# Scores of four heads in one TensorE block, a hidden layer in two PSUM banks, and V of two heads split at once

## The chip, the cores and the metric

One NeuronCore of a Trainium2 chip runs one program. The metric is the time of one execution on the device in microseconds (us). The engines that matter are TensorE (PE, with its weight loads as PEld), VectorE (DVE), ScalarE (ACT) and the sync engine (SP), which issues nearly all the DMAs. A matmul's result lands in PSUM, which has eight banks of 512 fp32 columns on each of 128 partitions.

## The reference

```
scores = q @ k.T / 8 + bias(head, distance)     # batch 4, 8 heads, 768 positions, head size 64
scores = where(first n_global keys or the last n_local, scores, -1e9)
x = softmax(scores) @ v                         # (4, 8, 768, 64) -> 3072 tokens x 512
h = x @ w_in                                    # 512 -> 2048
g = max(h, 0) + alpha * min(h, 0)
out = g @ w_out                                 # 2048 -> 512, fp32
```

## The kernel before, in words

**Tiles.** The 3072 tokens are worked off in 12 units `u` of 256 tokens, three to a batch. A unit has attention for 8 heads (`attend`) and the two layers. Keys outside a local window and 32 global columns are never computed: a query block of 128 has 256 key columns, or 128 where it is a batch's first; so a head's scores are two windows of 256 columns, or, in units 0, 3, 6 and 9, one of 128 and one of 256. Each head's scores take one PSUM bank.

**Precision.** Values are split into two fp16 parts (ScalarE or VectorE makes the high part, VectorE the rest), and each product is three fp16 matmuls. From unit 4 on (`QU`) this holds for scores too: one block is 12 matmuls of 64 contraction rows (line 627), two heads at once, one in rows 0 to 63 of the array and one in rows 64 to 127. All other matmuls use all 128 rows.

**Attention of a head.** Scores; bias, mask and row minimum in one VectorE instruction per window (line 650); exp on ScalarE (655); probabilities split (`ps`, lines 347/348 and 367); a DMA transposes them into `vp`, the buffer that holds the head's split V as well (697, 699); two heads' values are multiplied in one TensorE block (711) into the bank `av`, four heads to a bank; VectorE scales the four heads into `xn` (722).

**First layer.** From unit 3 on `ff_in4` makes four feature blocks by a Strassen-like scheme: seven products of 12 matmuls (829) into three partial sums X, Y and Z. The order is X (B11), Z (B21), Y (T1), X (T2), Y (B22), X (T3), X (T4). X and Y come from the two `h` banks in turn, Z from the bank `ax`. ScalarE takes copies of X and Y on the way (`take`, 837), VectorE joins Z and Y with copies (`join`, 840), applies alpha (865), and the result is split into `ghl` (872, 366). `ff_out` multiplies it by the second layer's weights (927). Unit 2 uses `ff_in2` instead, which puts two feature blocks in the two halves of one bank (896) and reads each half on its own.

**PSUM.** `sp` 2 banks (scores), `av` 1, `ax` 1, `h` 2, `o` 2: all eight.

**Order.** The program is a static order per engine. Every operation is given to `Plan` with a key (a place in time, counted in slots of which a unit has 16), its reads and writes, and a guessed cost. `Plan.order` simulates the engines: each takes the ready operation with the lowest key whose buffers are free. Operations are emitted in the order of their planned starts, and semaphores are set by the tile framework from that order. Keys that matter: scores of head h at `begin(u) + 2h`, its values at 5.5 after its pair's second head; `ff_in4` at the unit's slot, `ff_out` of block f `GLAG` slots behind. `FLEX` says when an engine takes over another's copy, `OWN` how long the plan lets a result age before the same engine uses it. The plan tracks the parts of a buffer that an operation names as separate.

Of the kernel before, what the change touches and what calls it, by code (L numbers as in the profile page):

```python
# [15 lines left out]
F16 = mybir.dt.float16  # L16
# [7 lines left out]
P = 128  # L24
# [7 lines left out]
UT = 256  # L32
# [7 lines left out]
XS, WI, WO, KG = 2.0**8, 2.0**8, 2.0**8, 2.0**-11  # L40
OSC = 1.0 / (XS * WI * WO * KG)
QS = 2.0**6
# [244 lines left out]
def c_dma(nbytes):  # L287
    return nbytes / 360.0
# [7 lines left out]
WIDE = 1  # L296
KP = 2
DP = 3.5
FLEX = {'ACT': 2, 'DVE': 1.5, 'POOL': 1}
GROUP = (2, 4, 4, 4)  # L300
PT4 = 0
DL = 3
# [6 lines left out]
WARM = 9  # L309
US = 3  # L310
QU = 4
LOADS = 1500
LANDS = 2500
OWN = {'PE': 0, 'DVE': 125}
SIGN = 6
QLEAD = 2
EV = 2
SLEAD = 36
SL = 3
GLAG = 6.5  # L320
SPARE = 600
CHECK = 140
RW = "abcd"
# [4 lines left out]
def fast(tc, cn, a):  # L328
    nc = tc.nc
    ctx = ExitStack()  # L330
    with ctx:
# [7 lines left out]
        def op(eng, key, cost, fn, r=(), w=(), spare=0):  # L339
            plan.op(key, r, w, (eng, cost, fn), spare=spare)  # L340

        def mul(key, out, src, by, r, w, first="ACT", n=None, psum=False):

            tile_ = hasattr(by, "t")
            ways = dict(
                ACT=("ACT", c_act(n, psum, tile_),
                     lambda: nc.scalar.mul(out=out(), in_=src(), mul=by.t if tile_ else by)),  # L347
                DVE=("DVE", c_dve(n, not psum, tile_), lambda: v.tensor_scalar(
                    out=out(), in0=src(), scalar1=by.t if tile_ else by, scalar2=None, op0=ALU.mult)),
            )  # L350
            plan.op(key, r, w, *[ways.pop(e) for e in (first, *[x for x in ways if x != first])])
# [8 lines left out]
        def rest(key, out, src, by, hi, r, w, n, first="DVE"):  # L360

            val = lambda: by.t if hasattr(by, "t") else by

            def on(e):
                if by is None:
                    return e.tensor_tensor(out=out(), in0=src(), in1=hi(), op=ALU.subtract)  # L366
                return e.scalar_tensor_tensor(out=out(), in0=src(), scalar=val(), in1=hi(), op0=ALU.mult,  # L367
                                              op1=ALU.subtract)

            ways = [("DVE", c_dve(n, False, hasattr(by, "t")), lambda: on(v))]  # L370
            if by is None and first == "POOL":
                ways.insert(0, ("POOL", c_pool(n), lambda: on(nc.gpsimd)))
            plan.op(key, r, w, *ways)


        def buf(tag, name, shape, dtype=F32):
            return Buf(plan, pools[tag], tag, shape, dtype, name)
# [159 lines left out]
        first, firstv = {}, {}  # L537
# [25 lines left out]
        def windows(u):  # L563

            if u % 3:
                return ((0, 0, 256, 0, 0), (1, 160, 256, 0, 256))
            return ((0, 0, 128, 256, 0), (1, 32, 256, 0, 128))

        xn, xt_, xt, group, pair, halves = {}, {}, {}, {}, {}, {}

        def scale_bias(h, key):
            op("ACT", key, c_act(384), lambda: nc.scalar.mul(out=Dh[h].t, in_=Dh[h].t, mul=QS**2), r=[], w=[Dh[h]])
# [1 line left out]
        def idle(u, h, tag, *others):  # L574

            return ((tag,) + others)[h % (1 + len(others))] if u == 0 else tag

        def attend(u, h, key):

            b, c = divmod(u, 3)  # L580
            nk = 416 if c else 288
            nb = 4 if c else 3
            nv, npr = 64 * nb, 128 * nb
            plain = u < 2
            late = not plain
            uh = f"{u}_{h}"

            kp = key - KP - (3 if late else 0)
            if u > 1 and h % 2 == 0:

                x = buf("qk", "qk" + uh, [P, 672])
                op("SP", kp - 4, c_dma(P * 4 * (256 + nk)), lambda: nc.sync.dma_start(
                    out=x.t[:, : 256 + nk], in_=a["qk"][u - 2, h // 2, :, : 256 + nk]), w=[x], spare=LOADS)
                y = buf("v", "v" + uh, [P, 512])
                op("SP", kp - 4 + (1 if late else 0), c_dma(P * 8 * nv), lambda: nc.sync.dma_start(
                    out=y.t[:, : 2 * nv], in_=a["vw"][u - 2, :, h * nv : (h + 2) * nv]), w=[y], spare=LOADS)
                for i in range(2):
                    first[u, h + i] = x, (lambda i=i: x.t[64 * i : 64 * i + 64, : 256 + nk])
                    firstv[u, h + i] = y, (lambda i=i: y.t[:, nv * i : nv * i + nv])
            rq, qk_ = first[u, h]  # L600
            rv, vrt = firstv[u, h]
            if u >= QU and h % 2 == 0:
                z = halves[u] = buf("qs", "qs" + uh, [P, 2, 672], F16)
                nq = 256 + nk
                mul(kp + QLEAD, lambda: z.t[:, 0, :nq], lambda: rq.t[:, :nq], QS, [rq], [(z, 0)], "ACT", nq)
                rest(kp + QLEAD, lambda: z.t[:, 1, :nq], lambda: rq.t[:, :nq], QS, lambda: z.t[:, 0, :nq], [rq, (z, 0)],
                     [(z, 1)], nq)
            if late:

                vp = buf("rd", "vp" + uh, [P, 2048], F16)  # L610
                rvh, rvl, rpt = (vp, 0), (vp, 1), (vp, 2)
                vhi, vlo, pflat = (lambda: vp.t[:, :256]), (lambda: vp.t[:, 256:512]), (lambda: vp.t[:, 512:1536])
                vv = lambda: vrt()[:, :nv]
                mul(kp + 3, lambda: vhi()[:, :nv], vv, XS, [rv], [rvh], "ACT", nv)
                rest(kp + 3, lambda: vlo()[:, :nv], vv, XS, lambda: vhi()[:, :nv], [rv, rvh], [rvl], nv)

            n2 = 1 if u == 2 or u == 3 and h < 4 else 2
            if h % n2 == 0:
                pair[u] = two = [buf(idle(u, h + i, "sp", "h"), f"sp{u}_{h + i}", [P, 512]) for i in range(n2)]

                def products(zz=halves.get(u)):
                    z = zz.t
                    for qb, off, n, _, pc in windows(u):
                        for m, (qi, ki) in enumerate(((0, 0), (0, 1), (1, 0))):
                            for i, sp in enumerate(two):
                                rows = slice(64 * i, 64 * i + 64)
                                nc.tensor.matmul(sp.t[:, pc : pc + n], lhsT=z[rows, qi, 128 * qb : 128 * qb + 128],  # L627
                                                 rhs=z[rows, ki, 256 + off : 256 + off + n], start=m == 0, stop=m == 2)

                def scores():  # L630
                    for i, sp in enumerate(two):
                        qk_ = first[u, h + i][1]
                        for qb, off, n, _, pc in windows(u):
                            nc.tensor.matmul(sp.t[:, pc : pc + n], lhsT=qk_()[:, 128 * qb : 128 * qb + 128],  # L634
                                             rhs=qk_()[:, 256 + off : 256 + off + n], start=True, stop=True)

                if u >= QU:
                    op("PE", key, 1.25 * npr + 200, products, r=[halves[u]], w=two)
                else:
                    op("PE", key, 1.67 * npr + 200, scores, r=[rq], w=two)  # L640
            sp = pair[u][h % n2]
# [5 lines left out]
            sm, av, works = group[u]  # L647

            for qb, _, n, dc, pc in windows(u):
# [3 lines left out]
                    r=[sp, Dh[h]], w=[(pr, qb), (sm, (n_, qb))])  # L653
            for qb, _, n, dc, pc in windows(u):
# [4 lines left out]
                    r=[(sm, (n_, qb))], w=[(pr, qb), (sm, (n_, 2 + qb))])  # L659
# [135 lines left out]
                         T2=(pick(a_, 10, 4), (a_, 1)), T3=(pick(b_, 0, 4), b_), T4=(pick(b_, 2, 4), b_),  # L795
                         B22=(pick(c_, 0, 2), c_))

        mo, acc = {}, {}

        def ff_in4(u, f4, key):  # L800

            x = xt[u]
            X, Y, Z = (buf(t, f"h{n}{u}_{f4}", [P, UT]) for t, n in (("h", "x"), ("h", "y"), ("ax", "z")))
            hs = buf("ra", f"hs{u}_{f4}", [P, 4, UT])
            ghl = buf("ra", f"ghl{u}_{f4}", [P, 2, 4 * UT], F16)
            kept = [buf("g", f"g{u}_{f4}_{i}", [P, 2 * UT]) for i in range(2)]
            snap = {n: (kept[i // 2], i % 2) for i, n in enumerate(("m1", "u2", "m5", "u3"))}
            two = lambda t: (t[0].t[:, UT * t[1] : UT * t[1] + UT] if isinstance(t, tuple) else t.t).rearrange(
                "p (q t) -> p q t", q=2)
            into = lambda i, t: hs.t[:, i::2, 128 * t : 128 * t + 128]  # L810

            def plain_w(i, half):
# [4 lines left out]
                return (lambda q, wi, c: sums[2 * f4 + q].t[:, wi, 256 * i + 128 * c : 256 * i + 128 * c + 128],  # L817
                        [(sums[2 * f4 + q], z) for q in range(2) for z in (i // 2, 2 + i // 2)])

            def product(k, bank, weights, name, begin, end):  # L820
                wt, rw = weights
                xp, rx = x[name]

                def go():
                    for q in range(2):
                        n = 0
                        for c in range(2):
                            for wi, xi in ((0, 0), (0, 1), (1, 0)):
                                nc.tensor.matmul(bank.t[:, 128 * q : 128 * q + 128], lhsT=wt(q, wi, c), rhs=xp(xi, c),  # L829
                                                 start=begin and q == n == 0, stop=n == 5,  # L830
                                                 skip_group_check=not (begin and q == 0))
                                n += 1

                op("PE", k, 12 * 55.6, go, r=[rx, *rw], w=[bank])

            def take(k, bank, out, w):
                op("ACT", k, c_act(UT, True), lambda: nc.scalar.mul(out=out(), in_=two(bank), mul=KG), r=[bank], w=w, spare=SPARE if u < NU - 1 else 0)  # L837
# [329 lines left out]
```

## Time and profile before

| what | value |
|---|---|
| median of 3 runs | 601.04 us (600.77 to 602.04) |
| profiled execution, its own time | 600.72 us |
| its span, first to last instruction | 598.9 us |
| TensorE busy | 584.8 us, 98% |
| VectorE busy | 502.9 us, 84% |
| ScalarE busy | 426.5 us, 71% |
| granted TensorE clock, mean | 0.996 |

In all rows times are microseconds from the span's start. A row of the timeline gives start, length, engine, line, operation, out<-in by tile name, shape and a count of merged instructions, and in brackets the engine's idle time before it with what ended it. Matmuls overlap in the pipeline: a row's length runs to the end of its last matmul, so the time that a block costs TensorE is read from its start to the next row's start.

### The profile page before, as it was taken

The numbers are of one execution on the slowest core, as the hardware profiler recorded it, in microseconds if no ns is written. First come the engines' busy times: TensorE is split into PE (matmuls) and PEld (weight loads), VectorE is DVE, ScalarE is ACT, GpSimd is POOL, SyncE is SP. The second block draws the span as 40 slices with busy tenths as digits, with TensorE's granted clock in tenths as the row PEclk, the third lists the DMA queues.
The fourth block names the chain that finished last, engine by engine and source line by source line (L and its number), as shares of the span: only waits on it lengthen the run. The fifth ranks groups of instructions, "written<-read, shape, count | busy, mean of one in ns | idle before, by whom it ended". The sixth has DMA issues, their size and how long they took to land.

```text
span 598.9 us, 16204 instructions
## 1 busy us (share of the span) xinstructions
PE 584.8 (98%) x6359; PEld 416.1 (69%) x6359; DVE 502.9 (84%) x1363; ACT 426.5 (71%) x1125; POOL 1.6 (0%) x11
## 2 busy tenths in 40 slices
PE   8999999999999999999999999999999999999994
PEld 7876666666667767777777777777777777777762
DVE  7999999999999999888799799788798798664441
ACT  6987999985687788677687788676586686542421
POOL 1000000000000000000000000000000000000000
PEclk9999999999999999999999999999999999999998
DMA  8996335346657339647568557567457536421001
GB/s 310 414 411 220 120 71 155 90 108 151 142 126 181 56 96 182 154 107 136 121 113 154 138 99 154 121 99 144 121 105 161 138 81 99 81 46 19 36 1 42
DMA packets 135397, 79.41 MB, mean 133 GB/s; under 512 B 116496, under 2 KB 118288, under 8 KB 135312
## 3 DMA queue, kind: packets, MB, share of 16 engines
q1 hardware_dynamic: 134592, 77.10, 53.8%
q8 instruction: 52, 0.85, 0.6%
q10 hardware_dynamic: 720, 1.18, 0.5%
q14 instruction: 33, 0.27, 0.2%
HBM read 43.79 MB, written 6.29 MB: 84 GB/s over the span
## 4 chain that ended last, share of the span: by engine, by line
PE 72%; DVE 18%; ACT 6%; issue 2%; DMA 1%; POOL 0%; POOLq 0%
PE o L927 33%; PE hx L829 15%; PE hy L829 7%; PE av L711 4%; PE hz L829 4%; PE h L896 4%; PE sp L627 3%; DVE pr L650 2%; DVE whl L367 2%; DVE wf L506 1%; DVE ws L529 1%; ACT pr L655 1%; DVE gg L366 1%; PE sp L634 1%; DVE g L905 1%
## 5 line engine op out<-in xcount | busy, mean ns | idle before, releaser
L927 PE MATMUL o<-whl,ghl 128*128 128x512 f16 x867 | 218.3, 379 | 1.6 <-DVE ghl L366 1.6
L829 PEld LDWEIGHTS <-sw 128*128 128x128 f16 x1728 | 104.7, 98 | 22.6 <-issue 0.2
L927 PEld LDWEIGHTS <-ghl 128*128 128x128 f16 x867 | 75.1, 98 | 64.3 <-issue 5.3
L655 ACT ACTIVATE pr<-pr,sm 128x256 f32<-128x256 f32 (+1 forms) x192 | 92.6, 484 | 12.3 <-DVE sm L650 11.9
L829 PEld LDWEIGHTS <-whl 128*128 128x128 f16 x1296 | 79.6, 98 | 20.7 <-issue 0.6
L837 ACT ACTIVATE g<-hx 128x256 f32<-128x256 f32 x108 | 41.0, 380 | 64.7 <-PE hx L829 64.1
L865 DVE SCALAR_TENSOR_TENSOR hs<-hs,alpha 128x256 f32<-128x256 f32 x144 | 65.8, 479 | 19.9 <-ACT hs L837 18.9
L650 DVE CUSTOM_DVE_ANT_0 pr<-sp,D 128x256 f32<-128x256 f32 (+1 forms) x192 | 70.1, 395 | 12.1 <-PE sp L627 10.6
L896 PE MATMUL h<-xt,whl 128*128 128x256 f16 x576 | 68.9, 273 | 1.0 <-DVE g L905 0.5
L927 PE MATMUL o<-whl,gg 128*128 128x512 f16 x288 | 67.8, 379 | 0.3 <-DVE gg L366 0.3
L896 PEld LDWEIGHTS <-whl 128*128 128x128 f16 x576 | 55.2, 98 | 14.6 <-issue 4.1
L367 DVE SCALAR_TENSOR_TENSOR ps<-pr,ps 128x512 f16<-128x512 f32 (+1 forms) x80 | 51.4, 644 | 5.7 <-ACT ps L347 5.6
L366 DVE TENSOR_TENSOR ghl<-hs,ghl 128x512 f16<-128x512 f32 x72 | 47.1, 685 | 2.2 <-ACT ghl L872 2.1
L927 PEld LDWEIGHTS <-gg 128*128 128x128 f16 x288 | 27.1, 98 | 30.2 <-issue 2.4
L872 ACT CAST ghl<-hs 128x512 f16<-128x512 f32 x72 | 41.7, 612 | 4.3 <-DVE hs L865 4.0
L655 ACT ACTIVATION_READ_ACCUMULATOR pr<-pr,sm 128x1 f32 x192 | 36.7, 191 | 0.0
L347 ACT ACTIVATE ps<-pr 128x512 f16<-128x512 f32 (+1 forms) x59 | 35.5, 601 | 1.1 <-DMA vp<-ps 0.2
L837 ACT ACTIVATE hs<-hx 128x256 f32<-128x256 f32 x36 | 13.6, 377 | 30.3 <-PE hx L829 30.2
L711 PEld LDWEIGHTS <-vp 128*128 128x128 f16 x888 | 30.5, 98 | 3.6
L711 PE MATMUL av<-vp 128*128 128x64 f16 x888 | 32.4, 193 | 0.0
L367 DVE SCALAR_TENSOR_TENSOR vp<-v,vp 128x256 f16<-128x256 f32 (+1 forms) x80 | 31.1, 395 | 0.0
L829 PE MATMUL hz<-xt,whl 128*128 128x128 f16 x432 | 30.0, 219 | 0.0
(135 smaller groups left out, 875.3 us busy)
## 6 DMA issues: line engine op xcount, KB each, us to landing
w<-in_w_dram SPq DMA_DIRECT2D x32, 512.0 KB, 8.1
qk<-in_qk_dram SPq DMA_DIRECT2D x28, 336.0 KB, 3.4
v<-in_vw_dram SPq DMA_DIRECT2D x28, 256.0 KB, 3.7
out_dram<-os SPq DMA_DIRECT2D x19, 256.0 KB, 3.6
qk<-in_qk_dram SPq DMA_DIRECT2D x12, 272.0 KB, 3.3
v<-in_vw_dram SPq DMA_DIRECT2D x12, 192.0 KB, 3.1
first<-in_first_dram SPq DMA_DIRECT2D x4, 464.0 KB, 5.1
first<-in_first_dram SPq DMA_DIRECT2D x4, 336.0 KB, 9.9
```

The source lines that it names most:

```text
L347: lambda: nc.scalar.mul(out=out(), in_=src(), mul=by.t if tile_ else by)),
L366: return e.tensor_tensor(out=out(), in0=src(), in1=hi(), op=ALU.subtract)
L367: return e.scalar_tensor_tensor(out=out(), in0=src(), scalar=val(), in1=hi(), op0=ALU.mult, op1=ALU.subtract)
L650: op("DVE", key, c_dve(n) + 10, lambda qb=qb, n=n, dc=dc, pc=pc: v.tensor_tensor_reduce(out=pr.t[:, pc : pc + n], in0=sp.t[:, pc : pc + n] ...
L655: op("ACT", key + 1, c_act(n, ptr=1) + 93, lambda qb=qb, n=n, pc=pc: nc.scalar.activation(out=pr.t[:, pc : pc + n], in_=pr.t[:, pc : pc + ...
L711: nc.tensor.matmul(out, lhsT=p_[:, 128 * j : 128 * j + 128], rhs=v_[:, 64 * j : 64 * j + 64], start=m == 0, stop=m == len(ps) - 1)
L829: nc.tensor.matmul(bank.t[:, 128 * q : 128 * q + 128], lhsT=wt(q, wi, c), rhs=xp(xi, c), start=begin and q == n == 0, stop=n == 5, skip_gr ...
L837: op("ACT", k, c_act(UT, True), lambda: nc.scalar.mul(out=out(), in_=two(bank), mul=KG), r=[bank], w=w, spare=SPARE if u < NU - 1 else 0)
L865: op("DVE", ks[4 + 2 * i], c_dve(UT, ptr=True), lambda n=n: v.scalar_tensor_tensor(out=hs.t[:, n, :], in0=hs.t[:, n, :], scalar=alpha[:, 4 ...
L872: op("ACT", ks[6], c_act(512), lambda q=q, cols=cols: nc.scalar.copy(out=ghl.t[:, 0, cols], in_=flat(q)), r=src, w=[(ghl, q)])
L896: nc.tensor.matmul(hp.t[:, cols], lhsT=w.t[:, wi, wc], rhs=x.t[:, NC * xi + c, :], start=n == 0, stop=n == 3 * NC - 1)
L927: nc.tensor.matmul(o.t[:, cols], lhsT=g_()[:, tok], rhs=w.t[:, wi, 512 + cols.start : 512 + cols.stop], start=f == 0 and n == 0, stop=f == ...
```

## The change

It changes three things, and four constants of the plan.

1. From unit 6 (`BATCH`) on, `attend` computes the scores of four heads in one TensorE operation of 24 matmuls instead of two operations of 12. The four banks are the two `sp`, `ax` and `av`. Both loads of q and k and both splits for the four heads are made ahead of that block.
2. `ff_in4` no longer allocates X, Y and Z for each group. Two whole `h` banks stay allocated: X alternates between the halves of the first, Y and Z are the halves of the second. A part named "group" orders products that begin or end a sum in one bank.
3. From unit 2 on V of two heads is split by one ScalarE and one VectorE operation of twice the width, into the even head's `vp`.
4. `FLEX['DVE']` 1.5 to 2.5, `OWN['DVE']` 125 to 2.5, `GLAG` 6.5 to 7.5; `BATCH = 6` is new.

```diff
-FLEX = {'ACT': 2, 'DVE': 1.5, 'POOL': 1}
+FLEX = {'ACT': 2, 'DVE': 2.5, 'POOL': 1}
+BATCH = 6
-OWN = {'PE': 0, 'DVE': 125}
+OWN = {'PE': 0, 'DVE': 2.5}
-GLAG = 6.5
+GLAG = 7.5
...
+                if not batch:
+                    load_qk(h, kp)
+                elif h % 4 == 0:
+                    load_qk(h, kp)
+                    load_qk(h + 2, kp + 1)
...
-                mul(kp + 3, lambda: vhi()[:, :nv], vv, XS, [rv], [rvh], "ACT", nv)
-                rest(kp + 3, lambda: vlo()[:, :nv], vv, XS, lambda: vhi()[:, :nv], [rv, rvh], [rvl], nv)
+                if h % 2 == 0:
+                    whole = lambda i: vp.t[:, 512 * i : 512 * i + 2 * nv]
+                    vsplit[u] = (vp, 0), (vp, 1), whole
+                    vv = lambda: y.t[:, : 2 * nv]
+                    mul(kp + 3, lambda: whole(0), vv, XS, [rv], [(vp, 0)], "ACT", 2 * nv)
+                    rest(kp + 3, lambda: whole(1), vv, XS, lambda: whole(0), [rv, (vp, 0)], [(vp, 1)], 2 * nv)
...
-            n2 = 1 if u == 2 or u == 3 and h < 4 else 2
+            n2 = 4 if batch else 1 if u < QU and (u == 2 or u == 3 and h < 4) else 2
             if h % n2 == 0:
-                pair[u] = two = [buf(idle(u, h + i, "sp", "h"), f"sp{u}_{h + i}", [P, 512]) for i in range(n2)]
+                tags = ("sp", "sp", "ax", "av") if batch else ("sp",) * n2
+                pair[u] = two = [buf(idle(u, h + i, tags[i], "h"), f"sp{u}_{h + i}", [P, 512]) for i in range(n2)]
+                zs = [halves[u, (h + i) // 2] for i in range(0, n2, 2)] if u >= QU else []
...
+                    for i0, z_ in enumerate(zs):
...
-                    op("PE", key, 1.25 * npr + 200, products, r=[halves[u]], w=two)
+                    op("PE", key, 1.25 * npr * len(zs) + 200, products, r=zs, w=two)
...
-            X, Y, Z = (buf(t, f"h{n}{u}_{f4}", [P, UT]) for t, n in (("h", "x"), ("h", "y"), ("ax", "z")))
+            if not banks:
+                banks.extend(buf("h", f"h{n}", [P, 2 * UT]) for n in "xy")
+            X, Y, Z = (banks[0], f4 % 2), (banks[1], 0), (banks[1], 1)
...
-                op("PE", k, 12 * 55.6, go, r=[rx, *rw], w=[bank])
+                op("PE", k, 12 * 55.6, go, r=[rx, *rw], w=[into_] + [(into_[0], "group")] * (begin or end))
```

## Rows read from the trace of the kernel before

**Rows 1.** Windows: length, busy us (instructions) of PE, PEld, DVE, ACT, POOL; clock; DMA
```profile
50.00:225.00 175.00, 172.26 (x1546) 116.25 (x1544) 172.49 (x421) 145.51 (x353) 0.00 (x0) 1.00 0.50 122
225.00:560.00 335.00, 335.00 (x4184) 241.62 (x4181) 271.50 (x764) 231.31 (x640) 0.00 (x0) 1.00 0.57 116
```
**Rows 2.** The page: the chain that ended last, share of the span by engine
```profile
PE 72%; DVE 18%; ACT 6%; issue 2%; DMA 1%; POOL 0%; POOLq 0%
```
**Rows 3.** Timeline of the last stretch: TensorE's final block
```profile
582.89 7.94 PE L927 MATMUL o<-whl,ghl 128*128 128x512 f16 x39
```
**Rows 4.** Timeline of TensorE around scores of two heads, windows of 256
```profile
341.10 0.83 PE L829 MATMUL hx<-xt,whl 128*128 128x128 f16 x12
341.87 0.83 PE L627 MATMUL sp<-qs 64*128 64x256 f16 x12
342.63 0.82 PE L927 MATMUL o<-whl,ghl 128*128 128x512 f16 x3
343.28 0.83 PE L829 MATMUL hz<-xt,whl 128*128 128x128 f16 x12
343.95 0.81 PE L927 MATMUL o<-whl,ghl 128*128 128x512 f16 x3
```
**Rows 5.** The same in unit 9: windows of 128 and 256
```profile
387.61 0.67 PE L627 MATMUL sp<-qs 64*128 64x128 f16 x12
...
409.99 0.67 PE L627 MATMUL sp<-qs 64*128 64x128 f16 x12
410.59 0.82 PE L927 MATMUL o<-whl,ghl 128*128 128x512 f16 x3
```
**Rows 6.** Line 627 over the whole span: durations min/median/max, first and last start
```profile
L627 PE MATMUL sp<-qs x384: 216/269/280, 163.7 to 512.6; 64*128 64x256 f16 x168, 64*128 64x128 f16 x24
```
**Rows 7.** Waits: engine line <- releaser: us in total, times, longest
```profile
PE o L927 <- DVE ghl L366: 1.6, 2, 1.4
```
**Rows 8.** Timeline around the longer of these two waits
```profile
222.45 0.68 DVE L366 TENSOR_TENSOR ghl<-hs,ghl 128x512 f16<-128x512 f32 x1
...
223.19 0.60 PE L927 MATMUL o<-whl,ghl 128*128 128x512 f16 x2 [1.39 <-DVE ghl L366]
```
**Rows 9.** Timeline of ScalarE and TensorE: two halves of one bank, unit 2
```profile
158.08 0.47 ACT L347 ACTIVATE g<-h,ak 128x256 f32<-128x256 f32 x1 [0.64 <-PE h L896]
...
153.95 4.09 PE L896 MATMUL h<-xt,whl 128*128 128x256 f16 x36
```
**Rows 10.** Timeline of VectorE and TensorE: join of Z, then product Y, three places
```profile
189.69 0.42 DVE L840 SCALAR_TENSOR_TENSOR hs<-hz,g 128x256 f32<-128x256 f32 x1
...
190.14 0.55 PE L829 MATMUL hy<-xt,sw 128*128 128x128 f16 x7
...
254.18 0.42 DVE L840 SCALAR_TENSOR_TENSOR hs<-hz,g 128x256 f32<-128x256 f32 x1
254.28 0.83 PE L829 MATMUL hy<-xt,sw 128*128 128x128 f16 x12
...
565.42 0.42 DVE L840 SCALAR_TENSOR_TENSOR hs<-hz,g 128x256 f32<-128x256 f32 x1 [0.48 <-PE hz L829]
...
565.79 0.72 PE L829 MATMUL hy<-xt,sw 128*128 128x128 f16 x10
```
**Rows 11.** Timeline: values of a group's last two heads, then its scaling
```profile
372.75 0.86 PE L711 MATMUL av<-vp 128*128 128x64 f16 x24
...
373.65 0.69 DVE L722 TENSOR_TENSOR xn<-av,sm 128x512 f32<-128x512 f32 x1
```
**Rows 12.** Timeline of SyncE: transposes of the heads scored at 341.87; all of them
```profile
347.16 2.77 SPq L697 DMA_TRANSPOSE vp<-ps  x2
...
DMA to landing us min/median/max: 2.5/3.5/5.8
```
**Rows 13.** Lines: a split of 256 columns and one of 512 on VectorE
```profile
L367 DVE SCALAR_TENSOR_TENSOR ps<-pr,ps 128x512 f16<-128x512 f32 (+1 forms) x80 | 51.4, 644 | 5.7 <-ACT ps L347 5.6
L367 DVE SCALAR_TENSOR_TENSOR vp<-v,vp 128x256 f16<-128x256 f32 (+1 forms) x80 | 31.1, 395 | 0.0
```

More of the change, by code (lines that the diff above doesn't have):

```diff
@@ L567, in windows @@
             return ((0, 0, 128, 256, 0), (1, 32, 256, 0, 128))
-        xn, xt_, xt, group, pair, halves = {}, {}, {}, {}, {}, {}
+        xn, xt_, xt, group, pair, halves, vsplit = {}, {}, {}, {}, {}, {}, {}
         def scale_bias(h, key):
@@ L588, in attend, with load_qk @@
             kp = key - KP - (3 if late else 0)
-            if u > 1 and h % 2 == 0:
-                x = buf("qk", "qk" + uh, [P, 672])
+            batch = u >= BATCH
+            def load_qk(h, kp):
+                x = buf("qk", f"qk{u}_{h}", [P, 672])
                 op("SP", kp - 4, c_dma(P * 4 * (256 + nk)), lambda: nc.sync.dma_start(
                     out=x.t[:, : 256 + nk], in_=a["qk"][u - 2, h // 2, :, : 256 + nk]), w=[x], spare=LOADS)
+                for i in range(2):
+                    first[u, h + i] = x, (lambda i=i: x.t[64 * i : 64 * i + 64, : 256 + nk])
+                if u >= QU:
+                    z = halves[u, h // 2] = buf("qs", f"qs{u}_{h}", [P, 2, 672], F16)
+                    nq = 256 + nk
+                    mul(kp + QLEAD, lambda: z.t[:, 0, :nq], lambda: x.t[:, :nq], QS, [x], [(z, 0)], "ACT", nq)
+                    rest(kp + QLEAD, lambda: z.t[:, 1, :nq], lambda: x.t[:, :nq], QS, lambda: z.t[:, 0, :nq], [x, (z, 0)],
+                         [(z, 1)], nq)
+            if u > 1 and h % 2 == 0:
+                if not batch:
[3 more added lines that the diff above has]
+                    load_qk(h + 2, kp + 1)
                 y = buf("v", "v" + uh, [P, 512])
@@ L597, in attend @@
                 for i in range(2):
-                    first[u, h + i] = x, (lambda i=i: x.t[64 * i : 64 * i + 64, : 256 + nk])
                     firstv[u, h + i] = y, (lambda i=i: y.t[:, nv * i : nv * i + nv])
@@ L601, in attend @@
             rv, vrt = firstv[u, h]
[L602 to L607, printed above, removed]
             if late:
                 vp = buf("rd", "vp" + uh, [P, 2048], F16)
-                rvh, rvl, rpt = (vp, 0), (vp, 1), (vp, 2)
-                vhi, vlo, pflat = (lambda: vp.t[:, :256]), (lambda: vp.t[:, 256:512]), (lambda: vp.t[:, 512:1536])
-                vv = lambda: vrt()[:, :nv]
-                mul(kp + 3, lambda: vhi()[:, :nv], vv, XS, [rv], [rvh], "ACT", nv)
-                rest(kp + 3, lambda: vlo()[:, :nv], vv, XS, lambda: vhi()[:, :nv], [rv, rvh], [rvl], nv)
@@ L617, in attend @@
-            n2 = 1 if u == 2 or u == 3 and h < 4 else 2
-            if h % n2 == 0:
-                pair[u] = two = [buf(idle(u, h + i, "sp", "h"), f"sp{u}_{h + i}", [P, 512]) for i in range(n2)]
[L621 to L628, printed above, removed]
+                rpt, pflat = (vp, 2), (lambda: vp.t[:, 1024:])
@@ new lines, in attend @@
+                if h % 2 == 0:
[4 more added lines that the diff above has]
+                    rest(kp + 3, lambda: whole(1), vv, XS, lambda: whole(0), [rv, (vp, 0)], [(vp, 1)], 2 * nv)
+                rvh, rvl, both = vsplit[u]
+                of_h = slice(nv * (h % 2), nv * (h % 2) + nv)
@@ new lines, in attend, with products @@
+                vhi, vlo = (lambda: both(0)[:, of_h]), (lambda: both(1)[:, of_h])
+            n2 = 4 if batch else 1 if u < QU and (u == 2 or u == 3 and h < 4) else 2
+            if h % n2 == 0:
+                tags = ("sp", "sp", "ax", "av") if batch else ("sp",) * n2
+                pair[u] = two = [buf(idle(u, h + i, tags[i], "h"), f"sp{u}_{h + i}", [P, 512]) for i in range(n2)]
+                zs = [halves[u, (h + i) // 2] for i in range(0, n2, 2)] if u >= QU else []
+                def products():
+                    for i0, z_ in enumerate(zs):
+                        z = z_.t
+                        for qb, off, n, _, pc in windows(u):
+                            for m, (qi, ki) in enumerate(((0, 0), (0, 1), (1, 0))):
+                                for i, sp in enumerate(two[2 * i0 : 2 * i0 + 2]):
+                                    rows = slice(64 * i, 64 * i + 64)
+                                    nc.tensor.matmul(sp.t[:, pc : pc + n], lhsT=z[rows, qi, 128 * qb : 128 * qb + 128],
+                                                     rhs=z[rows, ki, 256 + off : 256 + off + n], start=m == 0, stop=m == 2)
@@ L796, in x_combine @@
                          B22=(pick(c_, 0, 2), c_))
-        mo, acc = {}, {}
+        mo, acc, banks = {}, {}, []
         def ff_in4(u, f4, key):
             x = xt[u]
-            X, Y, Z = (buf(t, f"h{n}{u}_{f4}", [P, UT]) for t, n in (("h", "x"), ("h", "y"), ("ax", "z")))
+            if not banks:
+                banks.extend(buf("h", f"h{n}", [P, 2 * UT]) for n in "xy")
+            X, Y, Z = (banks[0], f4 % 2), (banks[1], 0), (banks[1], 1)
+            bank = lambda b: b[0].t[:, UT * b[1] : UT * b[1] + UT] if isinstance(b, tuple) else b.t[:, :UT]
             hs = buf("ra", f"hs{u}_{f4}", [P, 4, UT])
@@ L807, in ff_in4 @@
             snap = {n: (kept[i // 2], i % 2) for i, n in enumerate(("m1", "u2", "m5", "u3"))}
-            two = lambda t: (t[0].t[:, UT * t[1] : UT * t[1] + UT] if isinstance(t, tuple) else t.t).rearrange(
-                "p (q t) -> p q t", q=2)
+            two = lambda t: bank(t).rearrange("p (q t) -> p q t", q=2)
             into = lambda i, t: hs.t[:, i::2, 128 * t : 128 * t + 128]
@@ L818, in sum_w, with product @@
                         [(sums[2 * f4 + q], z) for q in range(2) for z in (i // 2, 2 + i // 2)])
-            def product(k, bank, weights, name, begin, end):
+            def product(k, into_, weights, name, begin, end):
                 wt, rw = weights
@@ L828, in go @@
                             for wi, xi in ((0, 0), (0, 1), (1, 0)):
-                                nc.tensor.matmul(bank.t[:, 128 * q : 128 * q + 128], lhsT=wt(q, wi, c), rhs=xp(xi, c),
+                                nc.tensor.matmul(bank(into_)[:, 128 * q : 128 * q + 128], lhsT=wt(q, wi, c), rhs=xp(xi, c),
                                                  start=begin and q == n == 0, stop=n == 5,
```

## The prediction

> **What bounds the kernel now.** I read four views, in this order. The table of stretches comes first, since shares over the whole span mix stages. From 225 to 560 us TensorE is busy for all 335.00 us, VectorE for 271.50 and ScalarE for 231.31; from 50 to 225 us TensorE has 172.26 of 175 and VectorE 172.49, so there the two bound together [rows 1]. The granted clock is 1.00 in both stretches, the 2.4 GHz level. The chain that ended last agrees: 72% of the span is TensorE's own work [rows 2]. After the last TensorE block, which ends at 582.89 + 7.94 = 590.83, 8.1 us of output remain to the span's end at 598.9, and no edit touches them [rows 3]. So from 50 us on time can come only from two places: what TensorE is charged as busy but does not need, and its 2.7 us without work before 225 us (175 - 172.26). The third view, the waits, names the largest part of these 2.7: TensorE's 927 waits for `ghl` twice, 1.6 us in all [rows 7]. The fourth is the timeline around a score block, which shows busy time that is no work.
>
> **The score block, priced.** A product of 12 matmuls of 128 columns normally takes 343.95 - 343.28 = 0.67 us from its start to the next start. The one ahead of a score block takes 341.87 - 341.10 = 0.77, so going in costs 0.10. The score block takes 342.63 - 341.87 = 0.76 for 12 matmuls of 256 columns, two at a time [rows 4]. In unit 9, with half of the matmuls at 128 columns, it takes 410.59 - 409.99 = 0.60 [rows 5]. There three of the six pairs are 128 columns shorter, which saves 0.16 us: 128 columns of a pair cost 0.053, six pairs of 256 cost 0.64, and 0.76 - 0.64 = 0.12 is left. A plain product shows a small step between matmuls (0.67 for 12 x 0.053 = 0.64, 2.5 ns each), some 0.015 for six pairs. Coming out costs about 0.105, and a block loses 0.10 + 0.105 = 0.20 us on its two edges. Line 627 has 384 matmuls, 32 blocks of 12 [rows 6]; units 6 to 11 have 24 of them, and the change makes 12. Twelve blocks' edges go: 12 x 0.20 = **2.4 us off TensorE**. Nothing hides this, since TensorE is the bound there. The seam inside the new block is not in the trace. It could cost nothing (within a block the weights already change six times per head at no visible price) or as much as the edges, which would leave nothing of the 2.4. I take nothing, since the nearest rows are the changes within one block, which alternate heads on the same row halves as the seam does.
>
> **GLAG, from 6.5 to 7.5.** Scores of unit 8 and of unit 9 start at 341.87 and 387.61 [rows 4, 5]: 45.7 us to a unit, 2.86 to a slot. `ff_out` moves back by that much behind `ff_in4` from unit 3 on. In the wait at 221.80 VectorE delivered `ghl` 1.39 us after TensorE had come to it [rows 8]; one slot covers that and the shorter one of 1.6 - 1.39 = 0.2. Bounds: all 2.7 us of idle go, or none, with new lateness in a redrawn order. I take 1.6, the two waits that this constant is about. Next late there is VectorE, full until 225 us, which a later `ff_out` can only relieve.
>
> **X, Y and Z in two banks.** TensorE's matmuls stay the same in number and shape. What is new is that B11 of a group writes into the bank from which ScalarE still takes T4 of the group before, and T1 (Y) into the bank from which VectorE joins Z. The plan counts halves as separate, so it makes no room for this. The trace shows what happens: at 157.44 ScalarE has nothing left and waits 0.64 us for a half of an `h` bank. TensorE is in a run of three products from 153.95 to 158.04, some 1.3 us each; the half wanted was the second's, done by then, but the read starts at 158.08, 0.04 after the third product, into the other half, has ended [rows 9]. So a read and a write of one bank wait for each other even on different halves, whichever was emitted second. The Trainium skill states the same as a rule that speaks against this edit: "PSUM — Partial Sum Buffer", section "PSUM bank collisions raise a hardware error", has software keep engines apart by bank, not by address; by it each of the 36 groups pays at both places. Where the write is emitted first, the reader loses up to a product, 0.67 us. VectorE, with 63 us free from 225 to 560, and ScalarE, with 104, have that; behind them wait `hs` and `ghl`, which now have a slot more. Where the read is emitted first, TensorE stands still, with everything queued behind it. Between product Z and product Y there is one `ff_out` step (0.65 us), which covers most of the join. In 36 groups the join starts before Y's start six times; the first, a middle one and the last stand in [rows 10]. There the join's end plus 0.04 passes Y's start by 0.01, 0.36 and 0.09 us. Over the six this makes 1.2 us. Bounds: nothing (Y always emitted first), and 36 x (0.42 + 0.04) = 16.6 us (every join starts just as Y is due). I take 1.2, the order that the rows show. A gain below nothing is excluded, since TensorE never waits for these banks after 225 us. T4's take costs TensorE nothing at the usual order, B11 directly behind T4.
>
> **`av` and `ax` as score banks.** `ax` is free once Z has left it. `av` is not: a four-head block can start only when the group ahead has been scaled out of `av`. Its key comes 8 slots after the previous one's, but the previous values have 6 + 5.5 = 11.5, so each block comes about 3.5 slots (10 us) late, and its own values 8 slots or 22.9 us after it. Two heads are scored at 341.87, their transposes are issued until 349.93 and land 3.5 us after their issue in the median [rows 12], some 11 us in all. Two more heads through the same engines add about 4. So 15 of 22.9, and lateness does not pile up. At the hand-over itself TensorE must wait for line 722: values start at 372.75, the scaling runs from 373.65 to 374.34 [rows 11], 1.59 us after that start, of which the values' own block takes 0.86 less the pipeline's 0.16 (as 0.83 against 0.67 in [rows 4]), 0.70. Bounds per block: nothing, if `ff` products stand between, and 0.89 plus what VectorE has queued ahead, if none do. I take nothing, because the plan sees this wait and has `ff` work ready. Behind a waiting score block all of TensorE's queue stands.
>
> **V and the rest, at nothing.** 80 splits of 395 ns on VectorE become 40 of some 644 [rows 13]: 5.8 us less work over the span, and a similar saving on ScalarE. After 225 us neither is the bound; before it some 2 us of VectorE's 172 go, which I leave as margin (bounds: 0 and 2 us gain). The second load of q and k and its split come about 3 slots earlier; SyncE issues as many DMAs as before, and the split's cover is ScalarE's and VectorE's free time. FLEX moves copies from VectorE to ScalarE; OWN lets dependent VectorE steps follow each other directly, where nothing else is ready. Both are taken at nothing, within the 2.7 us above for a gain, and for a loss within the same 2.7.
>
> **Sum.** -2.4 - 1.6 + 1.2 = -2.8 us against the profiled execution's 600.72: 597.9. That execution lies 0.3 below the median 601.04, so on the median's footing the forecast is **598.2 us**.
>
> **Rivals.** *The waits come back.* The order of the whole program is redrawn, and VectorE is full until 225 us. For it: one late `ghl` cost 1.4 us. Against it: the added slot. Then -2.4 + 1.2: 599.8. *Bank sharing is the new wait.* If the redrawn order puts the join just ahead of Y in most groups, the price is 36 x 0.23 (the mean of 0 and 0.46) = 8.3, and -2.4 - 1.6 + 8.3 gives 605.3. For it: [rows 9], and joins that start within 0.1 us of Y [rows 10]. Against it: 30 of 36 joins start after Y. By the skill's rule above this is the case to expect wherever the order puts the read first. *The hand-over of `av`, the case on the other side.* TensorE stands at each of the 12 blocks until VectorE has scaled the group ahead. From (2.8 + 1.2) / 12 = 0.33 us each the kernel is slower beyond doubt. With all of 0.89 exposed: 10.7 - 2.8 = 7.9, 608.9; with half, 603.6. For it: the block is overdue by its key and will be put at the first moment the plan allows, with no slack against VectorE's real lateness. Against it: before, the bank of the next scores was free long ahead. *The seam costs an edge.* Then the 2.4 stay where they are: 600.6.
>
> **How the numbers follow.** Forecast 0.55, waits come back 0.14, bank sharing 0.15, hand-over 0.11, seam 0.05. The forecast's own range is 595.9 (601.04 - 2.4 - 2.7, all early idle gone) to 599.8. The 8-in-10 range runs to 603.6, the half-exposed hand-over; above it lie most of bank sharing's and half of the hand-over's chance, some 0.16, and 0.03 below. A measurement tells 0.2%, 1.2 us, from no change: faster means under 599.8. That is the forecast and half of the waits' case, 0.62; within 0.2%: the other half, the seam, and bank sharing at a small price, 0.17; slower 0.21.
>
> **What would show it.** Right: in units 6 to 11 blocks of 24 scores of about 1.40 us (1.09 in units 6 and 9) with one pair of edges; no wait of 927 for `ghl` above a few tenths; TensorE's busy time down by some 2.4; line 829's waits for the join about 1 us in all. Wrong: score blocks with idle time ahead of them released by line 722; 829 (Y) released by 840 in most groups; a gap between the block's two halves; VectorE or ScalarE waiting so long for products that 927 waits for `ghl` again.

## The result, and the profile after

The changed kernel takes 606.98 us (605.87 to 609.49, 6 runs) against 601.3 in the same comparison: ratio 1.0097, interval 1.0082 to 1.0113. It is slower by 5.7 us; the forecast was 598.2, the range ended at 603.6. The profiled execution took 607.55, its span is 605.8.

The first view is the table of stretches (columns as in [rows 1]), with the stretch from 94 to 151 us in the kernel before and in the changed one, and three short stretches of the changed one around its longest wait.

```profile
50.00:225.00 175.00, 171.68 (x1530) 116.09 (x1528) 167.02 (x394) 140.56 (x332) 0.00 (x0) 0.99 0.49 120
225.00:560.00 335.00, 331.07 (x4132) 239.16 (x4130) 268.54 (x714) 230.09 (x637) 0.00 (x0) 1.00 0.57 115
...
94.00:151.00 57.00, 56.71 (x451) 36.90 (x449) 56.03 (x143) 46.97 (x118) 0.00 (x0) 1.00 0.49 115
94.00:151.00 57.00, 55.17 (x433) 36.41 (x430) 52.44 (x127) 43.94 (x107) 0.00 (x0) 0.97 0.54 127
...
138.00:142.00 4.00, 2.17 (x14) 1.24 (x12) 4.00 (x16) 3.12 (x9) 0.00 (x0) 1.00 1.21 225
142.00:146.50 4.50, 4.50 (x28) 3.40 (x27) 1.40 (x3) 0.17 (x1) 0.00 (x0) 0.62 0.61 228
146.50:151.00 4.50, 4.50 (x55) 3.80 (x52) 3.42 (x7) 4.50 (x13) 0.00 (x0) 1.00 0.21 47
```

TensorE, busy throughout from 225 to 560 us before [rows 1], is idle there for 3.9 us. And after it stood for 1.83 us at the start of unit 2 the granted clock averages 0.62 for 4.5 us, that is, mostly the lower level, 1.2 GHz. The timeline of TensorE shows the wait, and a score block of four heads later:

```profile
138.61 1.39 PE L653 MATMUL sp<-qk 64*128 64x128 f32 x8
141.83 1.51 PE L917 MATMUL h<-xt,whl 128*128 128x256 f16 x9 [1.83 <-DMA xt<-xs]
...
308.39 1.48 PE L646 MATMUL sp<-qs 64*128 64x256 f16 x24
309.81 0.84 PE L850 MATMUL hx<-xt5b,whl 128*128 128x128 f16 x12
```

A block of four heads takes 309.81 - 308.39 = 1.42 us, where two of [rows 4] take 1.52 and pay 0.10 more on a second way in. The waits of TensorE (line, releaser, us, times, longest) are now:

```profile
PE h L917 <- DMA xt<-xs: 1.8, 1, 1.8
PE hx L850 <- ACT hs L858: 1.7, 5, 0.6
...
PE av L730 <- DMA vp<-ps: 1.1, 1, 1.1
PE hy L850 <- DVE hs L861: 1.0, 2, 0.6
...
PE o L948 <- DVE ghl L367: 0.8, 1, 0.8
```

A measure of where time goes is the start of the same `ff_out` matmul in both traces, counted in the order in which they run. The 99th starts at 94.63 before and at 93.89 after (0.75 early), the 195th, in the first product of unit 2, at 146.39 and 151.23 (4.84 late). TensorE ends at 590.83 and 597.03 (6.2 late). Not all of the 4.84 is lost, since the changed kernel has by then run 12 more matmuls of 256 columns and 18 more of values, some 1.8 us of work. Lost are 1.5 us of idle time (1.83 from 94 to 151 us, against 0.29) and 1.7 by the lower clock. From 225 to 560 us come another 3.9 us of idle time, less the 2.4 that the score blocks save. So the larger part of the net loss falls between 94 and 151 us, where neither the four-head blocks (from 264 us) nor the two shared banks (from 186 us) exist yet. What exists there is attention of unit 2, with the joint split of V, and the new constants. The timeline shows its pace: scaling of its first four heads on VectorE, and the first values on TensorE (before, then after).

```profile
99.50 0.68 DVE L722 TENSOR_TENSOR xn<-av,sm 128x512 f32<-128x512 f32 x1
...
84.01 0.86 PE L711 MATMUL av<-vp 128*128 128x64 f16 x24
```
```profile
110.36 0.69 DVE L741 TENSOR_TENSOR xn<-av,sm 128x512 f32<-128x512 f32 x1
...
92.75 0.51 PE L730 MATMUL av<-vp 128*128 128x64 f16 x12
```

The listing of SyncE's instructions in the built program (names without the unit's number) gives the reason. In the changed kernel the transposes of unit 2 are issued for heads 0, 2, 1, 4, 3, 6, 5, 7; the first five:

```
L716 DMA_TRANSPOSE vp_0_715<-ps_0_1067 128x8x128
L716 DMA_TRANSPOSE vp_2_1022<-ps_2_1215 128x8x128
L716 DMA_TRANSPOSE vp_1_1303<-ps_1_1131 128x8x128
L716 DMA_TRANSPOSE vp_4_1390<-ps_4_1396 128x8x128
L716 DMA_TRANSPOSE vp_3_1507<-ps_3_1311 128x8x128
```

A buffer's place in its pool's queue is the key of its first use, and `fits` lets only the front be taken. Before, each head's `vp` is first used by its own V split, at its key less 2. Now an odd head's `vp` is first used by its transpose, at its key plus 2. With heads two slots apart that is 2h - 2 for an even head h and 2h + 2 for an odd one: the queue runs 0, 2, 1, 4, 3, 6, 5, 7. `rd` has four buffers. Head 1 cannot start its transpose until head 2 has taken a buffer, and head 3 not until head 4 has, by when all four are gone; it waits for the values of heads 0 and 1. SyncE's rows show that. Before, the transposes of heads 0, 1 and 2 start at 73.15 and after, and that of head 3 at 91.93 (first two rows). After, that of head 1 is the third, at 87.32, and that of head 3 the fifth, at 103.70, after TensorE's values at 92.75.

```profile
73.15 13.77 SPq L697 DMA_TRANSPOSE vp<-ps  x3
...
91.93 1.25 SPq L697 DMA_TRANSPOSE vp<-ps  x1
```
```profile
69.61 1.35 SPq L716 DMA_TRANSPOSE vp<-ps  x1
...
82.43 1.25 SPq L716 DMA_TRANSPOSE vp<-ps  x1
87.32 1.75 SPq L716 DMA_TRANSPOSE vp<-ps  x1
...
97.22 1.23 SPq L716 DMA_TRANSPOSE vp<-ps  x1
...
103.70 1.23 SPq L716 DMA_TRANSPOSE vp<-ps  x1
```

### The profile page after: what moved, and what is told of

Same layout as the page of the kernel before. It is cut to its first block, busy times and chain, and to the rows that moved or that the text cites. A ratio compares the mean times of both kernels' runs of the same rounds, so it can differ in the third digit from the quotient of the medians.

```text
span 605.8 us, 16117 instructions
## 1 busy us (share of the span) xinstructions
PE 586.0 (97%) x6359; PEld 417.3 (69%) x6359; DVE 497.4 (82%) x1296; ACT 425.6 (70%) x1112; POOL 1.6 (0%) x11
## 4 chain that ended last, share of the span: by engine, by line
PE 71%; DVE 18%; ACT 4%; issue 3%; DMA 3%; ACTq 0%; DVEq 0%
PE o L948 32%; PE hx L850 14%; PE hy L850 10%; PE h L917 7%; PE av L730 4%; PE sp L646 2%; DVE pr L669 2%; PE sp L653 2%; DMA vp<-ps 2%; DVE xs L367 1%; DVE xn L741 1%; DVE gg L367 1%; DVE wf L507 1%; DVE ps L368 1%; DMA xt<-xs 1%
## 5 line engine op out<-in xcount | busy, mean ns | idle before, releaser
L917 PE MATMUL h<-xt,whl 128*128 128x256 f16 x576 | 70.5, 277 | 2.8 <-DMA xt<-xs 1.8
L669 DVE CUSTOM_DVE_ANT_0 pr<-sp,D 128x256 f32<-128x256 f32 (+1 forms) x192 | 68.5, 398 | 4.3 <-PE sp L646 2.3
L861 DVE SCALAR_TENSOR_TENSOR hs<-hy,g 128x256 f32<-128x256 f32 x72 | 30.4, 422 | 33.8 <-PE hy L850 30.6
L348 ACT ACTIVATE ps<-pr 128x512 f16<-128x512 f32 (+1 forms) x75 | 44.1, 588 | 5.5 <-DMA vp<-ps 4.8
L850 PE MATMUL hx<-xt,whl 128*128 128x128 f16 x432 | 30.0, 219 | 1.7 <-ACT hs L858 1.7
L850 PE MATMUL hy<-xt,sw 128*128 128x128 f16 x432 | 30.0, 219 | 0.6 <-DVE hs L861 0.6
```

The source lines that it names most:

```text
L669: op("DVE", key, c_dve(n) + 10, lambda qb=qb, n=n, dc=dc, pc=pc: v.tensor_tensor_reduce(out=pr.t[:, pc : pc + n], in0=sp.t[:, pc : pc + n] ...
L850: nc.tensor.matmul(bank(into_)[:, 128 * q : 128 * q + 128], lhsT=wt(q, wi, c), rhs=xp(xi, c), start=begin and q == n == 0, stop=n == 5, sk ...
L917: nc.tensor.matmul(hp.t[:, cols], lhsT=w.t[:, wi, wc], rhs=x.t[:, NC * xi + c, :], start=n == 0, stop=n == 3 * NC - 1)
```

## The experiments

Each was timed beside the kernel before, five rounds; a ratio is to it, with its interval. Theory A is the buffer order just told. Theory B is the constants, C bank sharing as the main loss; D is that the waits at shared banks can be planned away.

**V alone.** The kernel before with the change's part 3 only (`BATCH = 99`, three banks, old constants).

> The kernel before with the joint split of V alone (old constants, pairs of heads, three banks for X, Y, Z). Theory A (the joint split delays attention of unit 2, because the odd head's vp now stands in the buffers' queue behind the next even heads' vp): TensorE is 4 to 5 us late at the end of unit 1's ff_out (151 instead of 146.4), waits for xt at the start of unit 2, and the kernel takes 604 to 606. Theory B (the constants redraw the order and cause the early loss): within 1 us of 601. Theory C (bank sharing alone is the loss): within 1 us of 601.

602.44 us, ratio 1.0027 (1.0016 to 1.0039): above what B and C expected, below what A did. Attention of unit 2 is late here too (first values at 97.37), but the loss that A puts behind it does not come: TensorE has other work until `xt` lands, and waits for it for 0.3 us, as before. The 195th `ff_out` matmul is 3.85 us late, but this execution waits 1.9 us for the first load at its very start, and has the same 1.8 us of extra work ahead of that matmul as the changed kernel; the two make nearly all of it. TensorE ends 2.07 late, about the wait at the start.

```profile
8.08 1.18 PE L653 MATMUL sp<-first 64*128 64x128 f32 x6 [1.91 <-DMA first<-in_first_dram]
...
PE h L915 <- DMA xt<-xs: 0.3, 1, 0.3
```

**All but V.**

```diff
-                if h % 2 == 0:
...
-                    mul(kp + 3, lambda: whole(0), vv, XS, [rv], [(vp, 0)], "ACT", 2 * nv)
...
+                mul(kp + 3, lambda: vhi()[:, :nv], vv, XS, [rv], [rvh], "ACT", nv)
```

> The changed kernel with V split per head as before; everything else of the change stays. Theory A: the early loss of 4.8 us goes, 601.5 to 603, since bank sharing still costs some 3 us and the larger score blocks give 2.4. Theory B: stays at 606 to 607. Theory C: stays at 606 to 607.

605.99 us, 1.0091 (1.0075 to 1.0106). The early loss does go: the 195th `ff_out` matmul starts at 145.41, 0.98 early. But TensorE ends 3.2 late all the same; its waits are for transposes into `vp` (2.1 us, two times, at 319 and 457 us), for T4's take (1.5) and for the join (1.5). A miss for A's time: from 252 to 570 us TensorE is idle for 3.8 us here and for 2.8 in the changed kernel, so in four-head units the separate splits cost no less than the joint one in its wrong order. Taking V out of the change thus gains only 1.0 us, and the two intervals overlap.

**V joint, buffers in the order of heads.** This takes the odd head's `vp` with the even one's, and so earlier, and leaves all else of the change.

```diff
-                vp = buf("rd", "vp" + uh, [P, 2048], F16)
+                vp = vsplit.pop((u, h), None) or buf("rd", "vp" + uh, [P, 2048], F16)
                 if h % 2 == 0:
+                    odd = vsplit[u, h + 1] = buf("rd", f"vp{u}_{h + 1}", [P, 2048], F16)
-                    mul(kp + 3, ..., [rv], [(vp, 0)], "ACT", 2 * nv)
+                    mul(kp + 3, ..., [rv], [(vp, 0), (odd, 0)], "ACT", 2 * nv)
```

> The changed kernel, still with the joint split, but the odd head's vp is taken together with the even one's, by the split itself, so that the order of the buffers' queue is that of the heads again. Theory A: the early loss goes as in the run without the joint split, 601 to 603, and the second group of unit 2 is scaled by 130 us instead of 132.2. If the joint split itself (later or longer instructions) is to blame and not the queue's order: 605 to 607.

**599.72 us, 0.9977 (0.9968 to 0.9986): faster than the kernel before, and 7.3 us faster than the change.** Transposes are issued for heads 0, 1, 2, 3 in turn; unit 2's first values run at 82.12 instead of 92.75, its groups are scaled at 99.21 and 128.32, the 195th `ff_out` matmul is 0.78 late with the extra work ahead of it, and there is no wait for `xt` of unit 2. The stretches, the transposes and the values of this version:

```profile
50.00:225.00 175.00, 174.06 (x1562) 117.67 (x1561) 171.76 (x408) 144.75 (x343) 0.00 (x0) 1.00 0.51 122
225.00:560.00 335.00, 333.25 (x4176) 241.49 (x4175) 267.92 (x719) 227.87 (x630) 0.00 (x0) 1.00 0.53 115
...
70.43 7.77 SPq L717 DMA_TRANSPOSE vp<-ps  x2
...
82.12 0.51 PE L731 MATMUL av<-vp 128*128 128x64 f16 x12
```

**The same in units 2 to 5 alone** (`if u < BATCH` around the two added lines):

> The changed kernel with vp taken in the order of heads in units 2 to 5 only. Theory A with its places (the version in order of heads everywhere gained 4.1 us up to the end of unit 1, nothing from there to 250 us, and some 2 us in units 6 to 11): 602 to 603.5, TensorE's last ff_out of unit 1 at 147 us, the waits for the transposes into vp after 300 us stay. If the whole gain sits in the four-head units: 606 to 607.

601.8 us, 1.0004 (0.9993 to 1.0015): 5.2 of the 7.3. **In units 6 to 11 alone:**

> The changed kernel with vp taken in the order of heads in units 6 to 11 only. Theory A with its places: 604 to 605.5, unit 1 ends at 151 us as in the changed kernel, no waits for the transposes into vp after 300 us. If the whole gain sits in unit 2: 607.

605.15 us, 1.0074 (1.0048 to 1.01): 1.8 of the 7.3. This interval overlaps the changed kernel's; that the late half counts is clearer from the 601.8 above against 599.72, whose intervals lie apart. The two add up to 7.0, and each leaves the other's waits where they were: with the order mended early, TensorE still waits for the transposes in the four-head units (first row); mended late, it still waits for `xt` (second).

```profile
PE av L734 <- DMA vp<-ps: 1.7, 2, 1.2
```
```profile
PE h L921 <- DMA xt<-xs: 2.0, 1, 2.0
...
141.98 5.41 PE L921 MATMUL h<-xt,whl 128*128 128x256 f16 x48 [1.99 <-DMA xt<-xs]
```

The last row is the place where the changed kernel's trace shows the lower clock. Here TensorE stands even longer, 1.99 us, and the same 48 matmuls then take 5.25 us (141.98 to 147.23) at a granted clock of 1.00. So the slower clock does not follow each such stop, and is no fixed part of what the order of the buffers costs.

**The constants alone** on the kernel before, all three together.

> The kernel before with the change's three constants alone (FLEX DVE 2.5, OWN DVE 2.5, GLAG 7.5). Theory A and C: 599.5 to 601.5, with the two waits for ghl shorter. Theory B: 604 to 606, late at the end of unit 1.

602.67 us, 1.003 (1.0018 to 1.0042). A miss for all three. The waits for `ghl` shrink, but only from 1.6 to 1.0 us, and others come up beside them:

```profile
PE o L927 <- DVE ghl L366: 1.0, 2, 0.7
PE hx L829 <- DVE hs L840: 0.8, 1, 0.8
PE av L711 <- DMA vp<-ps: 0.8, 2, 0.4
```

**Two banks alone** on the kernel before.

> The kernel before with X, Y and Z in two banks alone: V split per head, pairs of heads, old constants. My forecast gave this edit +1.2 us: 602 to 603, with TensorE waiting for the join (840 before) about 1 us in all. Rival (bank sharing is the main loss): 604 to 607. Rival (nothing): 600.5 to 601.3.

602.86 us, 1.0023 (1.0011 to 1.0035), 1.4 us slower by the ratio. It is near the size that I gave the edit, but not all of it is the join: that wait is 0.8 us in all, and one for `ghl` stands beside it as before.

```profile
PE o L943 <- DVE ghl L367: 1.6, 1, 1.6
...
PE hy L845 <- DVE hs L856: 0.8, 2, 0.6
```

**Joint split in the right order alone** on the kernel before.

> The kernel before with the joint split, vp taken in the order of heads, old constants, pairs, three banks. Theory A (it was the queue's order, not the split): 600 to 601.3, and the run with the joint split alone (602.4) lost its 1.6 us by the order. If the wider split costs of itself: 602 to 603.

602.87 us, 1.0025 (1.0005 to 1.0046), with runs from 599.88 to 605.79. A said that the right order makes the split harmless everywhere; on the kernel before it does not: TensorE waits 1.5 us for `xt` of unit 2 here too. So the order of the buffers explains the changed kernel, not every kernel with a joint split. With the old constants the wait is even the other way round: 0.3 us in the wrong order (V alone), 1.5 in the right one.

**Pairs of heads**, `BATCH = 99`, on the version at 599.72.

> The version at 599.7 us with scores of two heads everywhere (joint split in the order of heads, two banks, new constants). My step 'twelve blocks' edges, 2.4 us': 602 to 602.5. If the larger blocks give back their 2.4 elsewhere: 599 to 600.5.

603.97 us, 1.0042 (1.0028 to 1.0056): without the larger blocks 4.2 us slower. The traces agree until about 246 us. The edges' 2.4 are in it; the rest lies in waits for the join, 3.5 us (six times) against 1.6 (three) with four heads. One of these, on TensorE and on VectorE:

```profile
296.79 0.81 PE L949 MATMUL o<-whl,ghl 128*128 128x512 f16 x3
298.12 0.83 PE L851 MATMUL hy<-xt,sw 128*128 128x128 f16 x12 [0.51 <-DVE hs L862]
...
297.65 0.41 DVE L862 SCALAR_TENSOR_TENSOR hs<-hy,g 128x256 f32<-128x256 f32 x1
```

`ff_out` is through by 297.45; the product into one half of the bank starts at 298.12, 0.06 after the join has read the other half (297.65 + 0.41). That is the price of one meeting in a shared bank: 0.67 us from start to start beyond its work.

**A plan that knows of the banks**, on the version at 599.72.

```diff
-    ..., r=[bank], w=w, ...)                       # take; join likewise
+    ..., r=[bank, (bank[0], "group")], w=w, ...)
```

> The version with the joint split and vp taken in the order of heads (599.7), and the plan told that a read of X, Y or Z and the start or end of a sum in the same bank exclude each other. Theory D (TensorE's waits for line 862, and 840 before, come from bank sharing that the plan does not see; in that version six of them, 0.5 to 0.7 us at their longest, some 1.6 us): the waits go, 597.5 to 598.5. If the waits are only one form of a chain that is late anyway, the time stays at 599 to 600.

607.2 us, 1.0095 (1.0075 to 1.0115). D fails: waits for the join fall from 1.6 to 0.6 us, but the order is redrawn, and two waits for transposes (2.0 us), four for `ghl` (1.5) and others take their place.

**X and Z in one bank, Y in the other, banks changing places from group to group**, on the same version.

```diff
-            X, Y, Z = (banks[0], f4 % 2), (banks[1], 0), (banks[1], 1)
+            one_, two_ = banks[f4 % 2], banks[1 - f4 % 2]
+            X, Y, Z = (one_, 0), (two_, 0), (one_, 1)
```

(Z's first matmul then goes without the flag that begins a sum, since X's product in the same bank has just carried it.)

> The version in the order of heads (599.7) with X and Z in the two halves of one bank, Y in the other bank, and the banks changing places from group to group: the join of Z and product Y no longer meet in a bank, nor T4's take and the next B11; the take after B11 and product Z now do. Theory D (TensorE's waits for the join are bank sharing): no wait of TensorE for the join, 598 to 599. If they are only exchanged for waits of product Z for the take: 599.5 to 601.

599.67 us, 0.9971 (0.996 to 0.9983), the same as without it. Y's waits for VectorE fall to 0.2 us, and X now has 1.3 (four times). The waits are exchanged.

**The same with the old constants.**

> The same with the three constants of the kernel before. The constants alone cost 1.8 us on the kernel before; if they cost as much here: 596.5 to 598. If each version has its own best constants and these belong to the new structure: 599 to 602.

604.96 us, 1.0057 (1.0038 to 1.0076): with `xt` of unit 2 late by 3.2 us. The constants cost 1.8 us on the old structure and are worth 5.3 on this one. They belong to the structure, and what a constant does cannot be read off one kernel for the other.

## Why the prediction was wrong

**The step that failed** is "V and the rest, at nothing". I counted the 80 splits that become 40, found VectorE's saving, and looked at who is the bound. I did not ask what else the removed instruction did. The odd head's split was the first use of its `vp`, and that first use set its place in the queue for four buffers. With it gone, attention of unit 2 gives its values 9 us later (92.75 against 84.0), its `xt` lands after TensorE has run out of other work, and TensorE stands for 1.83 us. In the profiled execution it then runs 48 matmuls of 256 columns in 6.92 us (141.83 to 148.75), where 109.2 ns each would make 5.24: 1.7 more through the clock. The median does not rest on these 1.7, since four of the six executions had a mean granted clock of 0.995 to 0.997 and still took 605.87 to 607.38. Mending the order gave 7.3 us back, 5.2 by units 2 to 5 and 1.8 by units 6 to 11, and left the change at -1.4 us by its ratio, half of the sum's -2.8. None of my rivals named it: they looked at PSUM, at the `ghl` waits and at the seam, and the list of what a moved step issues stopped at instructions and did not reach buffers.

**The sum of the other terms failed too.** With V split per head the rest of the change costs 5.5 us by its ratio and does not gain 2.8. TensorE's waits for transposes, T4's take and the join make 5.1 us there, where the sum has 1.2 for the join and nothing for the others. The joint split in the wrong order costs this kernel no more than separate splits; in the right order it is worth 6.3 us beside them (599.72 against 605.99). So the sum gave each part a price of its own, and the runs show that a part's price hangs on the others. What makes the waits of the version without V is not isolated.

**Right: the edges.** Blocks of 1.42 and, in units 6 and 9, 1.10 us against 1.40 and 1.09 expected; the seam costs nothing. It is worth 2.4 us as priced, and more where it also thins out the meetings in shared banks (4.2 without them).

**Right in mechanism, not in size: the two banks.** +1.2 forecast, +1.4 measured alone. That the two agree is in part luck: the waits for the join alone are 0.8, and each of the other three edits tried alone costs the kernel before as much, 1.5 to 1.8. A read of one half and a write into the other do wait for each other, as [rows 9] said. The Trainium skill ("PSUM — Partial Sum Buffer", section "PSUM bank collisions raise a hardware error") has software keep engines apart by bank and not by address. This case's traces agree with it: 0.06 us from the end of the read to the start of the product. One term failed: I put T4's take at nothing, since B11 stood right behind T4; in the new order there are five waits for it, 1.7 us in all, which with 1.0 for the join makes 2.7 in the changed kernel.

**Wrong in size: GLAG, -1.6.** In the changed kernel the waits for `ghl` are 0.8 us instead of 1.6, on the kernel before with the constants 1.0, and what was saved came up as other waits. The bound "none of it" was the better value. That the lateness comes from further up, so that moving one end of a wait only moves the wait, is argued and not shown.

**Right: the hand-over of `av`.** No score block waits for the scaling of the group ahead. The rival did not come.

**What stays open.** Why each part alone costs the old kernel 1.4 to 1.8 us is not settled beyond the waits listed, nor why TensorE's wait for `xt` of unit 2 goes with the order of the buffers under the new constants (1.8 and 2.0 us in the wrong order, 0.3 or none otherwise) and against it under the old ones (0.3 in the wrong order, 1.5 and 3.2 in the right one). The three constants were never moved one by one. Every edit redraws one static order, and the two versions meant as improvements (the plan that knows of banks, the old constants) lost 7.5 and 5.3 us through waits in new places. Those are argued from their waits alone and were not isolated.

## What to carry to other kernels

When an edit removes or merges an instruction, list what that instruction was first at: the first writer of a buffer fixes where the buffer stands in an allocator's or planner's queue, and a merged first use can turn that order round without a single slower instruction. Look in the listing of the queue that fills the buffers (here the order of heads in SyncE's transposes) before looking at engines. And where one static order ties all together, time a part both alone and in its company: the constants here were worth -1.8 us in one structure and +5.3 in the other.

## What the runs showed of the hardware

A stop of TensorE of 1.83 us, behind eight fp32 score matmuls of 64 rows, was followed by a mean granted clock of 0.62 over 4.5 us. At the same place and behind the same eight matmuls, stops of 1.47 us (joint split in the right order alone), 1.99 us (order mended late) and 3.20 us (banks in turn, old constants) were followed by a granted clock of 1.00. At the start of the program a wait of 1.91 us (V alone) was followed by a granted clock of 0.55 from 8 to 10 us and 0.60 from 10 to 12, one of 1.3 us (pairs of heads) by 1.00. So the length of the stop does not settle it, and these traces do not show what does. In the changed kernel the lower clock cost 1.7 us, about as much as the wait of 1.83 ahead of it. Going over to matmuls in two row halves and back costs 0.10 us each way, whether 12 matmuls stand between or 24: the second 12 add 1.42 - 0.76 = 0.66 us to a block and nothing to its edges.
